# A cross network of six layers: four sums of a middle layer's state made by accumulating DMAs in place of VectorE

## The chip, the core and the metric

The kernel runs on one core of one Trainium2 chip. The metric is the device time of one launch in microseconds (us), given as the median of several runs. Beside it there is a trace of one profiled execution; all durations below come from that trace.

## What is computed

The reference is a deep cross network on 16384 rows of 1024 bf16 values, with six layers. The state starts as x0; each layer multiplies the state by its own 1024x1024 weight, adds a bias, multiplies the result element by element with x0 and adds the old state:

```python
B, Din, L = 16384, 1024, 6
x = x0
for l in range(L):
    proj = jnp.einsum('bd,de->be', x, ws[l]) + bs[l]
    x = x0 * proj + x
return x
```

The last line of the loop is what the change is about: the sum of the new product and the old state.

## The kernel before

**Tiling.** The 16384 rows are cut into 16 pairs of two blocks of 512 rows. The state of a pair is held transposed in SBUF, 128 partitions by (n, k, b): n is the block (0 or 1), k one of eight slices of 128 features, b the row. Its two halves of features are called eh = 0 (k 0 to 3) and eh = 1 (k 4 to 7). So a state has four quarters of 128x2048 values (512 KB in bf16), one for each n and eh.

**Loops.** The outer loop `s` runs over eight outer steps, each with two pairs, called side A and side B. Inside it `l` runs over the six layers, and in each layer first A and then B is a step: 96 steps in all. The two sides alternate so that one side's last sums can be made while TensorE works on the other.

**Strassen products.** In each step the 2x2 block product of features by blocks of rows is made in Winograd's way from seven products instead of eight, numbered by `pid` (1, 2, 3 on parts of the state itself; 5, 6, 7, 4 on differences of them, the tiles `T13`, `T2` and `T4`). From the second outer step on, products 2 and 4 are in turn made from seven smaller ones, on differences in the tiles `ti2` and `ti4`. `mm` (L403) issues a product's matmuls of 128x512, `inner` (L411) those of 128x256. ScalarE brings the results from PSUM to the SBUF tiles P1s, S53 (the profile's S), P5s, U2s, C2 (the profile's cb), ea, eb and e4.

**The sums of a state.** Four products with x0 and four sums with the old state make the new state `xst` of a pair:
- quarter (n 0, eh 0) from P1s, by `m0` and `a0` near the end of the pair's own step;
- quarter (n 1, eh 0) from S53, by `m1` and `a1` in the following step, which is the other side's;
- quarters (n 1, eh 1) and (n 0, eh 1) from the two halves of C2, by one product and one sum over both, `mC2` and `aC2`, also in the following step.

`trail(Y, store)` returns the operations of the previous pair Y that are still to be made; `fin_of` gives a product and a sum of one quarter. In layers after the first the old state and the new one are the same tile (`X.src = X.xst` at a step's end), so the sum is made in place.

**Order.** All engines keep the order in which the program issues (`keep_in_program_order`). A step of VectorE goes: T13 of the step's own side; then the previous pair's operations mixed with T2, T4 and the ti4 differences, in the order of the list at L441; then the sums of ea and eb, and P1s + ea; then, by the list at L556, the ti2 differences of the other side's next step mixed with m0 and a0; then U2s + S53. The ti2 differences of the next step read the quarter (n 0, eh 1) that `aC2` has written in this step; the other side's T13 at the head of the next step reads the other three quarters.

**Buffers.** P1s, S53, P5s and U2s have one buffer each, C2 has two. So ScalarE can't fill P1s in a step before the product and the sum of the step before have read it. The weights are in a ring of nine tiles of 512 KB, one for each `pid` and for the two inner sets; SP loads the next layer's tile into a slot as soon as side B has used it. SP also loads the next x0 with transposing DMAs (from the second outer step to the seventh in layers 2 and 3, side A), and turns and writes finished states in the steps of layers 5 and 0. GpSimd issues nothing after the first few us.

Of the kernel before, what the change touches and what calls it, by code (L numbers as in the profile page):

```python
# [8 lines left out]
ADD = mybir.AluOpType.add  # L9
SUB = mybir.AluOpType.subtract  # L10
MULT = mybir.AluOpType.mult
# [6 lines left out]
def kernel(  # L18
# [7 lines left out]
    nc = tc.nc  # L26
    P = nc.NUM_PARTITIONS
    B, D = x0.shape
    L = ws.shape[0]
    KD = D // P  # L30
    KH = KD // 2
# [11 lines left out]
    pin = tc.keep_in_program_order  # L43

    def vtt(out, in0, in1, op):
        return pin(nc.vector.tensor_tensor(out=out, in0=in0, in1=in1, op=op))  # L46

    def vcopy(out, in_):
        return pin(nc.vector.tensor_copy(out=out, in_=in_))
# [23 lines left out]
    def evt(name):  # L73
        return ev_pool.tile([P, KH, NB], BF16, name=name)
# [47 lines left out]
    def combo(l, pid):  # L122
        if pid <= 7:
            a, op, b = {5: (lambda: raw12[l], ADD, lambda: W[0, l, 4]), 6: (lambda: W[0, l, 5], SUB, lambda: W[0, l, 1]),
                        3: (lambda: W[0, l, 2], SUB, lambda: W[0, l, 6]), 7: (lambda: W[0, l, 1], SUB, lambda: raw12[l])}[pid]
            if pid == 5:
                W[0, l, 5] = ei_pool.tile([P, KH, H], BF16, name=("eb", "e4")[l % 2])
            t = W[0, l, pid]
            vtt(t[:], a()[:], b()[:], op)
        else:  # L130
            w = W[0, l, {8: 2, 9: 4}[pid]]
            t = W[0, l, 8] if pid == 8 else ti_pool.tile([P, KH, H], BF16, name="ti4")
            i11, i12, i21, i22 = w[:, 0:2, 0:HE], w[:, 0:2, HE:H], w[:, 2:4, 0:HE], w[:, 2:4, HE:H]
            iv = t[:].rearrange("p k (j e) -> p k j e", e=HE)
            vtt(iv[:, 0], i12, i22, ADD)
            vtt(iv[:, 3], i11, i12, SUB)
            vtt(iv[:, 1], iv[:, 0], i11, SUB)
            vtt(iv[:, 2], i21, iv[:, 1], SUB)
        pin(nc.sync.dma_start(lc(l, pid), t[:]))

    def sub4(t):
        return {(i, j): t[:, 2 * i:2 * i + 2, j * NQ:(j + 1) * NQ] for i in range(2) for j in range(2)}

    def inner_t(hold, src, name):

        def t02():
            ti = ti_pool.tile([P, 4, 2, NQ], BF16, name=name)
            setattr(hold, name, ti)
            b = sub4(src())
            vtt(ti[:, 0], b[0, 1], b[0, 0], SUB)  # L150
            vtt(ti[:, 2], b[1, 1], b[0, 1], SUB)

        def t1():
            ti = getattr(hold, name)
            vtt(ti[:, 1], sub4(src())[1, 1], ti[:, 0], SUB)

        def t3():
            ti = getattr(hold, name)
            vtt(ti[:, 3], sub4(src())[1, 0], ti[:, 1], SUB)

        return [t02, t1, t3]
# [96 lines left out]
    def half(eh):  # L258
        return slice(eh * KH, (eh + 1) * KH)

    def trail(Y, store):

        if Y is None:
            return [None] * 7
        C2, E4, e5 = Y.C2, Y.E4, Y.e5
        eh1 = lambda t: t[:, :, KH:KD, :]
        m1, a1 = fin_of(Y, Y.C12, 0, 1)

        def s4():
            for i in range(2):  # L270
                vtt(E4[:, 2 * i:2 * i + 2, NQ:NB], E4[:, 2 * i:2 * i + 2, (1 - i) * NQ:(2 - i) * NQ], e5[:], ADD)

        def a1s():
            a1()
            if store:
                store_half(Y, 0)

        return [m1, lambda: vtt(C2[:, 1], C2[:, 1], Y.P5s[:], ADD), a1s,
                s4 if E4 is not None else None,
                (lambda: vtt(C2[:, 0], C2[:, 0], E4[:], ADD)) if E4 is not None else None,  # L280
                lambda: vtt(C2[:], C2[:], eh1(Y.x0T), MULT),
                lambda: vtt(eh1(Y.xst), C2[:], eh1(Y.src_in), ADD)]

    def fin_of(Y, C, eh, n):
        xs = half(eh)
        return [lambda: vtt(C, C, Y.x0T[:, n, xs, :], MULT),
                lambda: vtt(Y.xst[:, n, xs, :], C, Y.src_in[:, n, xs, :], ADD)]

    def fin_rows(X, C, n, eh, js=slice(0, KH), state=None):
# [17 lines left out]
    def store_half(Y, eh):  # L307
        ks = half(eh)
        for n in range(2):
            pin(nc.sync.dma_start_transpose(out=Y.x0T[:, n, ks, :].rearrange("p k (j r) -> p (k j) r", r=P),  # L310
                                            in_=Y.xst[:, n, ks, :].rearrange("r k b -> r (k b)")))
        with nc.allow_non_contiguous_dma(reason="256B runs"):
            for n in range(2):
                r0 = Y.pr * PR + n * NB
                for j in range(KH):
                    pin(nc.sync.dma_start(
                        out[r0 + j * P:r0 + (j + 1) * P, eh * H:(eh + 1) * H].rearrange("p (k r) -> p k r", r=P),
                        Y.x0T[:, n, ks, j * P:(j + 1) * P]))
# [12 lines left out]
    for s in range(NPAIR // 2):  # L331
        for l in range(L):
            for side in ("A", "B"):
                X, Y = cur[side], prev
                first, last = step == 0, (X.pr, l) == LAST
                in2, in4 = not first, s > 0 and not (s + 1 == NPAIR // 2 and l + 1 == L)
                psA, psX = ps[step % 2], ps[1 - step % 2]
                step += 1
                bias = lambda eh, m, l=l: b_all[:, l * KD + eh * KH + m: l * KD + eh * KH + m + 1]
# [83 lines left out]
                        abias(dst[:, m, :], pts[m][:], bias(eh, m))  # L423

                ended = Y is not None and Y.l == L - 1
                m1, s11, a1, s4, e4, mC2, aC2 = trail(Y, ended and last)
                if not first:
                    X.T13()
                P1s = evt("P1s")
# [8 lines left out]
                ev(P1s, pA, 0, 0)  # L438
                t2, t4 = (None, None) if first else (X.T2, X.T4)
                i02, i1, i3 = inner_t(X, lambda: X.T[4], "ti4") if in4 else [None] * 3  # L440
                for f in (m1, s11, a1, t2, s4, t4, e4, i02, mC2, i1, aC2, i3):  # L441
                    if f is not None:
                        f()
                if in2:
# [4 lines left out]
                    P5s, S53 = evt("P5s"), evt("S53")  # L449
# [53 lines left out]
                else:  # L503
# [20 lines left out]
                    P5s, S53 = evt("P5s"), evt("S53")  # L524
# [24 lines left out]
                if first:  # L549
                    combo(0, 8)  # L550
                m0, a0 = fin_of(X, P1s[:], 0, 0)
                j02, j1, j3 = inner_t(N, lambda: N.rhs(2), "ti2") if need2 else [None] * 3
                if last:
# [24 lines left out]
                U2s = evt("U2s")  # L578
                X.E4 = X.e5 = X.defer = None
                C2 = cb_pool.tile([P, 2, KH, NB], BF16, name="cb")  # L580
                X.C2, X.P5s, X.l = C2, P5s, l
                if in4:
                    w4, w4i, w7 = weights(4), weights(9), weights(7)
                    wj, wr4 = w4i[:].rearrange("p k (j e) -> p k j e", e=HE), sub_w(w4, HE)
                    b4, t4 = sub4(X.rhs(4)), X.ti4
                    E4 = X.E4 = ei_pool.tile([P, KH, NB], BF16, name="e4")
                    X.e5 = ei_pool.tile([P, 2, NQ], BF16, name="e5")
                    e4 = sub4(E4)
# [104 lines left out]
```

## Time and profile before

| | us |
|---|---|
| median of 3 runs | 2268.25 (2268.05 to 2268.64) |
| the profiled execution, its own time | 2268.03 |
| its span in the trace | 2266.2 |
| TensorE busy | 2259.2 (100%) |
| VectorE busy | 2161.6 (95%) |
| ScalarE busy | 1910.9 (84%) |
| GpSimd busy | 0.7 |
| DMA, share of 16 engines (SP's queue) | 51.7% |
| granted TensorE clock | 1.00 of full speed |

The span is the time from the first to the last instruction in the trace; 1.8 us of the execution lie around it. An engine's idle time matters only where the chain of work that ended last runs through it. A step's length can be read from one `T<-big 128x4096` of VectorE, the T13 at the head of each step, to the next.

### The profile page before, as it was taken

The numbers are of one execution on the slowest core, as the hardware profiler recorded it, in microseconds if no ns is written. First come the engines' busy times: TensorE is split into PE (matmuls) and PEld (weight loads), VectorE is DVE, ScalarE is ACT, GpSimd is POOL, SyncE is SP. The second block draws the span as 40 slices with busy tenths as digits, with TensorE's granted clock in tenths as the row PEclk, the third lists the DMA queues.
The fourth block names the chain that finished last, engine by engine and source line by source line (L and its number), as shares of the span: only waits on it lengthen the run. The fifth ranks groups of instructions, "written<-read, shape, count | busy, mean of one in ns | idle before, by whom it ended". The sixth has DMA issues, their size and how long they took to land.

```text
span 2266.2 us, 33559 instructions
## 1 busy us (share of the span) xinstructions
PE 2259.2 (100%) x12925; PEld 1264.4 (56%) x12925; DVE 2161.6 (95%) x2394; ACT 1910.9 (84%) x3307; POOL 0.7 (0%) x6
## 2 busy tenths in 40 slices
PE   9999999999999999999999999999999999999999
PEld 4555555555555555555555555555555555555554
DVE  8999989999999999999999999999999999999999
ACT  6777788888888888888888888888888888888887
POOL 0000000000000000000000000000000000000000
PEclk9999999999999999999999999999999999999999
DMA  7423494523945239442494434944348443483337
GB/s 231 151 94 121 149 216 159 146 85 119 255 133 136 93 124 257 132 121 97 128 259 122 121 112 127 245 121 121 125 124 236 121 131 121 126 228 121 104 119 178
DMA packets 508452, 334.59 MB, mean 148 GB/s; under 512 B 390530, under 2 KB 470404, under 8 KB 508292
## 3 DMA queue, kind: packets, MB, share of 16 engines
q1 hardware_dynamic: 508292, 332.45, 51.7%
q8 instruction: 101, 1.65, 0.3%
q14 instruction: 59, 0.48, 0.1%
HBM read 213.92 MB, written 52.43 MB: 118 GB/s over the span
## 4 chain that ended last, share of the span: by engine, by line
PE 99%; DMA 0%; DVE 0%; SPq 0%; issue 0%; ACT 0%; DVEq 0%
PE px L403 74%; PE px L411 24%; PE px L398 1%; DMA wp<-in_ws_dram 0%; DVE cb L46 0%; SPq L120 0%; DVE eb L46 0%; DVE T L46 0%; DVE wp L46 0%; SPq L217 0%; PE px L395 0%; PE px L393 0%; ACT cb L52 0%; SPq L220 0%; DVEq L46 0%
## 5 line engine op out<-in xcount | busy, mean ns | idle before, releaser
L403 PEld LDWEIGHTS <-wp 128*128 128x128 bf16 x7344 | 718.5, 98 | 669.9 <-issue 0.8
L403 PE MATMUL px<-T,wp 128*128 128x512 bf16 x4384 | 1069.4, 379 | 0.0
L403 PE MATMUL px<-big,wp 128*128 128x512 bf16 x2960 | 712.4, 379 | 0.4 <-ACT big L52 0.4
L411 PEld LDWEIGHTS <-wp 128*128 128x128 bf16 x4752 | 465.0, 98 | 254.3
L55 ACT ACTIVATE cb<-px,b_all 128x512 bf16<-128x512 f32 x760 | 502.0, 686 | 85.3 <-PE px L403 71.4
L411 PE MATMUL px<-ti,wp 128*128 128x256 bf16 x2684 | 402.7, 273 | 0.0
L52 ACT CAST ea<-px 128x512 bf16<-128x512 f32 x344 | 201.6, 586 | 140.5 <-PE px L411 140.5
L46 DVE TENSOR_TENSOR T<-big 128x4096 bf16<-128x4096 bf16 (+1 forms) x97 | 220.1, 2269 | 71.0 <-PE px L403 71.0
L52 ACT CAST U2s<-px 128x512 bf16<-128x512 f32 x384 | 225.0, 586 | 64.4 <-PE px L403 61.4
L55 ACT ACTIVATE P1s<-px,b_all 128x512 bf16<-128x512 f32 x380 | 254.3, 695 | 6.0 <-PE px L403 4.4
L55 ACT ACTIVATE S<-px,b_all 128x512 bf16<-128x512 f32 x380 | 242.3, 703 | 0.8 <-PE px L403 0.8
L46 DVE TENSOR_TENSOR T<-big,T 128x2048 bf16<-128x2048 bf16 x192 | 234.1, 1219 | 1.4
L52 ACT CAST P5s<-px 128x512 bf16<-128x512 f32 x384 | 217.9, 596 | 17.7 <-PE px L403 17.5
L46 DVE TENSOR_TENSOR cb<-cb,big 128x4096 bf16<-128x4096 bf16 (+2 forms) x105 | 221.6, 2113 | 0.7 <-ACT cb L52 0.5
L46 DVE TENSOR_TENSOR big<-cb,big 128x4096 bf16<-128x4096 bf16 x95 | 217.2, 2286 | 0.5
L52 ACT CAST e<-px 128x512 bf16<-128x512 f32 x328 | 192.7, 588 | 0.0
L411 PE MATMUL px<-big,wp 128*128 128x256 bf16 x1084 | 162.6, 273 | 0.0
L52 ACT CAST eb<-px 128x512 bf16<-128x512 f32 x258 | 152.1, 590 | 6.2
L411 PE MATMUL px<-T,wp 128*128 128x256 bf16 x984 | 134.2, 273 | 0.0
L46 DVE TENSOR_TENSOR P1s<-P1s,big 128x2048 bf16<-128x2048 bf16 x106 | 129.3, 1220 | 3.3 <-ACT P1s L55 2.4
L46 DVE TENSOR_TENSOR S<-U2s,S 128x2048 bf16<-128x2048 bf16 (+1 forms) x97 | 117.2, 1208 | 2.5 <-ACT U2s L52 2.4
L46 DVE TENSOR_TENSOR S<-S,big 128x2048 bf16<-128x2048 bf16 (+1 forms) x99 | 118.5, 1197 | 0.1
(77 smaller groups left out, 1360.8 us busy)
## 6 DMA issues: line engine op xcount, KB each, us to landing
wp<-Lc SPq DMA_DIRECT2D x252, 512.0 KB, 4.6
wp<-in_ws_dram SPq DMA_DIRECT2D x144, 512.0 KB, 3.4
out_dram<-big SPq DMA_DIRECT2D x28, 1024.0 KB, 10.7
Lc<-big SPq DMA_DIRECT2D x15, 512.0 KB, 2.7
Lc<-wp SPq DMA_DIRECT2D x9, 512.0 KB, 2.7
ea<-in_ws_dram SPq DMA_DIRECT2D x6, 512.0 KB, 5.2
Lc<-ti SPq DMA_DIRECT2D x6, 512.0 KB, 3.1
big<-in_x_dram SPq DMA_DIRECT2D x1, 2048.0 KB, 9.9
```

What stands on the lines that cost most here:

```text
L46: return pin(nc.vector.tensor_tensor(out=out, in0=in0, in1=in1, op=op))
L52: return pin(nc.scalar.copy(out=out, in_=in_))
L55: return pin(nc.scalar.activation(out=out, in_=in_, func=IDENT, bias=bias, scale=1.0))
L398: nc.tensor.matmul(pt, lhsT=rhs[:, k, m * P:(m + 1) * P], rhs=wt[:, k, :], start=(start and k == 0 and pid != 1), stop=(k == KH - 1), **kw)
L403: nc.tensor.matmul(pts[m][:], lhsT=wt[:, k, m * P:(m + 1) * P], rhs=rhs[:, k, :], start=(start and k == 0), stop=(k == KH - 1), **kw)
L411: nc.tensor.matmul(dst(m), lhsT=w[:, k, m * P:(m + 1) * P], rhs=rhs[:, k, :], start=(start and m == 0 and k == 0), stop=(k == 1), skip_gro ...
```

## The change

In layers 1 to 4 each of the four sums becomes a DMA that GpSimd issues. Its source is the product, its destination the quarter of the state, and it adds what it brings to what is there. The two products on the halves of C2 are made one by one instead of together, each directly behind the operation that completes its half, and each is followed by its own DMA; so the product of half 0 stands ahead of the ti4 differences, where the common product stood among them. The sum a1 has become a DMA directly behind m1, and a0 one at its old place between the ti2 differences. Layers 0 and 5 keep VectorE's sums: in layer 0 the old state is x0 in another tile, and layer 5 goes on to the output.

In the rebuilt order of the engines TensorE, ScalarE and SP issue the same instructions in the same order as before, and GpSimd issues 256 further DMAs of 128x2048, four in each of 64 steps.

```diff
+    def dadd(out, in_):
+        return pin(nc.gpsimd.dma_start(out=out, in_=in_, accum_op=ADD))
...
     def trail(Y, store):
...
-        return [m1, lambda: vtt(C2[:, 1], C2[:, 1], Y.P5s[:], ADD), a1s,
+        mul = lambda n: vtt(C2[:, n], C2[:, n], Y.x0T[:, n, KH:KD, :], MULT)
+        acc = lambda n: dadd(Y.xst[:, n, KH:KD, :], C2[:, n])
+
+        def m2():
+            mul(1)
+            acc(1)
+
+        def m3():
+            mul(0)
+            acc(0)
+
+        dma = by_dma(Y)
+        return [m1, a1s if dma else None, lambda: vtt(C2[:, 1], C2[:, 1], Y.P5s[:], ADD), m2 if dma else None, None if dma else a1s,
                 s4 if E4 is not None else None,
-                (lambda: vtt(C2[:, 0], C2[:, 0], E4[:], ADD)) if E4 is not None else None,
-                lambda: vtt(C2[:], C2[:], eh1(Y.x0T), MULT),
-                lambda: vtt(eh1(Y.xst), C2[:], eh1(Y.src_in), ADD)]
+                (lambda: vtt(C2[:, 0], C2[:, 0], E4[:], ADD)) if E4 is not None else None, m3 if dma else None,
+                None if dma else lambda: vtt(C2[:], C2[:], eh1(Y.x0T), MULT),
+                None if dma else lambda: vtt(eh1(Y.xst), C2[:], eh1(Y.src_in), ADD)]
+
+    def by_dma(Y):
+        return 0 < Y.l < L - 1
 
     def fin_of(Y, C, eh, n):
         xs = half(eh)
         return [lambda: vtt(C, C, Y.x0T[:, n, xs, :], MULT),
+                (lambda: dadd(Y.xst[:, n, xs, :], C)) if by_dma(Y) else
                 lambda: vtt(Y.xst[:, n, xs, :], C, Y.src_in[:, n, xs, :], ADD)]
...
-                m1, s11, a1, s4, e4, mC2, aC2 = trail(Y, ended and last)
+                m1, d1, s11, m2, a1, s4, e4, m3, mC2, aC2 = trail(Y, ended and last)
...
-                for f in (m1, s11, a1, t2, s4, t4, e4, i02, mC2, i1, aC2, i3):
+                for f in (m1, d1, s11, m2, a1, t2, s4, t4, e4, m3, i02, mC2, i1, aC2, i3):
```

In what follows d1 is the DMA behind m1 (from S53), d2 and d3 those behind the products on the halves 1 and 0 of C2, and d0 the one that stands for a0 (from P1s).

More of the change, by code (lines that the diff above doesn't have):

```diff
@@ L263, in trail @@
         if Y is None:
-            return [None] * 7
+            return [None] * 10
         C2, E4, e5 = Y.C2, Y.E4, Y.e5
@@ L336 @@
                 in2, in4 = not first, s > 0 and not (s + 1 == NPAIR // 2 and l + 1 == L)
+                X.l = l
                 psA, psX = ps[step % 2], ps[1 - step % 2]
@@ L580 @@
                 C2 = cb_pool.tile([P, 2, KH, NB], BF16, name="cb")
-                X.C2, X.P5s, X.l = C2, P5s, l
+                X.C2, X.P5s = C2, P5s
                 if in4:
```

## The prediction

> **What bounds the kernel now.** I read the page first, then one step of VectorE and of ScalarE in the timeline, then the DMA share by windows, then the DMA issues. The page:
>
> ```profile
> PE 2259.2 (100%) x12925; PEld 1264.4 (56%) x12925; DVE 2161.6 (95%) x2394; ACT 1910.9 (84%) x3307; POOL 0.7 (0%) x6
> ...
> PE 99%; DMA 0%; DVE 0%; SPq 0%; issue 0%; ACT 0%; DVEq 0%
> ```
>
> TensorE is busy for 2259.2 of 2266.2 us and carries 99% of the chain that ended last. What VectorE gives up can therefore buy at most the 7.0 us in which TensorE is idle, all of it, by the windows, in the first 30.5 (28.12 busy) and the last 55.2 us (50.58). VectorE is nearly as full. One step of it (layer 3, side A) in the timeline, start and duration in us:
>
> ```profile
> 995.27 2.29 DVE L46 TENSOR_TENSOR T<-big 128x4096 bf16<-128x4096 bf16 x1 [0.84 <-PE px L403]
> ...
> 999.75 1.22 DVE L46 TENSOR_TENSOR big<-S,big 128x2048 bf16<-128x2048 bf16 x1
> ...
> 1008.17 2.28 DVE L46 TENSOR_TENSOR big<-cb,big 128x4096 bf16<-128x4096 bf16 x1
> ...
> 1015.11 1.22 DVE L46 TENSOR_TENSOR big<-P1s,big 128x2048 bf16<-128x2048 bf16 x1
> ...
> 1018.65 2.29 DVE L46 TENSOR_TENSOR T<-big 128x4096 bf16<-128x4096 bf16 x1 [0.84 <-PE px L403]
> ```
>
> A step lasts 23.38 us (995.27 to 1018.65), as nearly all steps do; VectorE waits in it for 0.84 us alone, for TensorE. The sums are the three forms that write big: 1.14 + 2.20 + 1.14 us from start to start (a 128x2048 takes 1.14, a 128x4096 2.20, two 128x512 0.67). ScalarE in that step:
>
> ```profile
> 998.38 1.27 ACT L55 ACTIVATE P1s<-px,b_all 128x512 bf16<-128x512 f32 x2
> ...
> 1002.64 0.59 ACT L52 CAST ea<-px 128x512 bf16<-128x512 f32 x1 [0.71 <-PE px L411]
> ...
> 1004.38 0.59 ACT L52 CAST ea<-px 128x512 bf16<-128x512 f32 x1 [0.17 <-PE px L411]
> ...
> 1008.47 0.69 ACT L55 ACTIVATE P1s<-px,b_all 128x512 bf16<-128x512 f32 x1
> ```
>
> P1s has one buffer: ScalarE fills it from 3.11 us after the step's T (998.38 - 995.27) to 13.89. The cast of ea at 1004.38 ends at 1004.97 and TensorE reuses its bank at 1005.04, so a late ScalarE stops TensorE once its idle 0.71 + 0.17 and that 0.07, 0.95 us, are used up. The DMA share (second number from the right) of the two steps of one layer, then of 10.9 to 16.9 us after T in a B step, in an A step of layers 2 and 3, and in one of layer 4:
>
> ```profile
> 784.85:808.23 23.38, 23.38 (x138) 13.31 (x137) 22.43 (x26) 20.10 (x36) 0.00 (x0) 1.00 0.40 135
> 808.23:831.61 23.38, 23.38 (x138) 13.29 (x137) 22.43 (x26) 20.10 (x36) 0.00 (x0) 1.00 0.19 68
> 1029.55:1035.55 6.00, 6.00 (x32) 2.99 (x31) 5.90 (x7) 5.65 (x12) 0.00 (x0) 1.00 0.91 298
> ...
> 1006.17:1012.17 6.00, 6.00 (x32) 2.99 (x31) 5.90 (x7) 5.65 (x12) 0.00 (x0) 1.00 0.72 158
> 1052.93:1058.93 6.00, 6.00 (x32) 2.99 (x31) 5.90 (x7) 5.65 (x12) 0.00 (x0) 1.00 0.01 3
> ```
>
> A layer's nine weight loads (512 KB each) take (0.40 + 0.19) x 23.38 = 13.8 us of all 16 engines, 1.53 each. They crowd into the middle of the B steps; in the A steps of layers 2 and 3 it is the transposing loads of the next x0. From issue to landing:
>
> ```profile
> wp<-Lc SPq DMA_DIRECT2D x252, 512.0 KB, 4.6
> ...
> Lc<-big SPq DMA_DIRECT2D x15, 512.0 KB, 2.7
> ```
>
> **What is removed.** In the 64 steps of layers 1 to 4, sums of 1.14 + 1.14 + 2.20 = 4.48 us leave VectorE; two 128x2048 products in place of one 128x4096 give back 0.08. Its idle time grows from 0.84 to 5.2 us a step. TensorE's, ScalarE's and SP's orders stay, so this alone is worth nothing.
>
> **What is added.** 256 accumulating DMAs of 512 KB, four a step, all in GpSimd's queue, each behind its own product; GpSimd has nothing else to do. In us after a step's T: product with S ends at 3.42 (d1 goes out), C2[1]'s at 5.69 (d2), C2[0]'s, now ahead of the inner T4 differences, at 2.20 + 3 x 1.14 + 1.14 (T2) + 0.67 + 1.14 (T4) + 1.14 + 1.22 = 10.9 (d3). Behind it VectorE does the ti4 differences (1.34), ea (1.13) and P1s + ea, which waits for P1s until 13.89, and comes at 15.03 to the ti2 differences of the other side's next step. These read the half of the state that d3 writes. This is the new wait: queued behind it are P1s x x0, whose DMA (d0) goes out 0.67 + 1.22 us later, U2s + S, and the next T; and ScalarE can't fill P1s in the next step, at 23.38 + 3.11 = 26.49, before d0 has read it.
>
> **The price of a wait.** Let L3 and L0 be the times from the product's end to the landing. Up to L3 = 15.03 - 10.9 = 4.1 nothing waits. Above it d0 lands at 10.9 + L3 + 1.89 + L0, and TensorE stops when this passes 26.49 + 0.95: when L3 + L0 is over 14.65 us, and by the excess, in each such step. The other deadlines are looser: VectorE's own circle (next T at 23.38, 3.64 us of work behind the wait) allows L3 = 8.9, S is refilled at 12.6 (d1 may take 9.2), d2 has until the next T. A weight tile is freed one step (23.38 us) ahead of its next use and lands in 4.6, so weights have some 18 us of cover; if that went, TensorE would wait for wp.
>
> **How long a landing takes.** No row shows an accumulating DMA. Fixed part: 2.7 (Lc<-big) less 1.53 of moving is 1.2 us; GpSimd's handing over lies between SP's issue of such a DMA (0.32 to 0.38) and SP's slowest (5.1 for a transposing load, 10.28 for two). I take 1.8, a third of the way, as the form is that of the former and the engine neither's: f = 3.0. Moving: the addend and the old state are both read, so between one copy, 1.53, and three, 4.6; I take the middle, two, c = 3.06. Where another queue has work, I let it take turns, so time doubles.
> - B steps (28, outer steps 1 to 7): d1 and d2 need 6.1, and loads 2.1 (share 0.28), of the 7.5 us ahead of d3, which starts 0.7 late; L3 = f + 2c + 0.7 = 9.8, L0 = f + c = 6.1, sum 15.9: 1.25 us over, 35 us in all.
> - A steps of layers 2 and 3 in outer steps 1 to 6 (12): loads fill the engines (share up to 1.14) until about 15, where d1 and d2 have had 5.5 of their 6.1; d3 moves to 18.7 and lands at 21.7: L3 = 10.8, L0 = 6.1, sum 16.9, 2.25 over, 27 us.
> - The 16 other A steps of outer steps 1 to 7: 2 x 6.1 = 12.2, hidden with 2.4 to spare. The first outer step, whose loads lie otherwise: 0 (at most 8 x 1.25 = 10).
>
> Sum 62 us on the profiled 2268.0 (span 2266.2 and 1.8 around it; the median is 2268.25): **2330**. With one copy all is hidden, 2268. With c = 4.0 the same sums give 5.95 over in the 40 steps, 238 us, 2506; with 4.6, 8.95 and 8.35 over there and 2.25 in the 16 free A steps, some 390 us, 2660. Below nothing the 7.0 us of idle TensorE are the limit.
>
> **A rule that gives another result.** The row is 2.7 us for a plain 512 KB. The Trainium skill (DMA: Bandwidth & Descriptors, section Anatomy of one DMA) fits a GpSimd-issued DMA as 2.0 us plus bytes over 436 GB/s; with both operands counted that makes an estimated 4.4 us, f = 2.0 and c = 2.4, and by it a B step's sum is 11.2 and nothing is lost. No run here shows such a DMA.
>
> **Rivals.**
> - *Hidden after all* (the other side): landings short enough that L3 + L0 stays under 14.65 everywhere; with f = 3.0 this holds in the B steps from c under 2.8, in the crowded A steps from 2.5. For it: the point lies just under my c, and the uncrowded steps have 2.4 us to spare. Against: six of the eight crossings of a layer cycle are crowded. 2268. The rule above gives this.
> - *The DMA engines fill up*: two steps need 13.8 + 8c of 46.76 us, so from c = 4.1 on the loads fall behind, whatever the waits. At 4.6: (50.6 - 46.76) / 2 = 1.9 us in 64 steps at the least, with the waits above 2390 to 2660. Against: a copy takes 1.53.
> - *GpSimd can hand over only while VectorE pauses*: nothing in the trace speaks on it, as GpSimd is idle. d3 would wait for 15.03 (4.1 later), d0 0.7: 4.8 more in each sum, 6.0 and 7.0 over in the crowded steps, 2.4 in the 16 free ones, 292 us: 2560. The Trainium skill (SBUF — State Buffer, section Summary: rules for kernel authors) has GpSimd's descriptor writing starved while VectorE runs in its 2x mode; the same page's section on interference exempts two-input operations, which is what these are.
> - *A gain*: only the 7.0 us; at the ends the layers are 0 and 5, which the change leaves out.
>
> **How the numbers follow.** Waits as summed, 0.44; hidden 0.27; engines full 0.16; handing over held up 0.10; gain 0.03. A change of 0.2% (4.5 us) is about what a measurement tells from none: faster 0.03, same 0.27, slower 0.70. The range reaches from 2265, hidden and a little less, to 2510, c of 4.0; the likeliest case alone holds 2275 to 2510.
>
> **What would show it.** Right: VectorE loses 4.5 us a step, its wait ahead of ti<-big is for the DMA, ScalarE waits at P1s for a DMA, and the steps of outer steps 1 to 7 longer than 23.38 us are the B steps and the A steps of layers 2 and 3. Wrong: all steps at 23.38 (hidden), TensorE waiting for wp (engines full), or landings over 10 us in the free A steps (handing over).

## The result, and the profile after

The changed kernel takes 2780.07 us (median of 4 runs, 2771.76 to 2809.77) against 2268.26 us before (4 runs, 2268.05 to 2268.64): a ratio of 1.228, with a 95% interval of 1.221 to 1.235. The prediction had the direction and named two of the three waits, but the loss is 512 us where it forecast 62, far beyond its range.

The page of the profiled execution (2771.76 us, span 2769.9); the lines that the change adds shift the numbers, so L424 and L432 are the former L403 and L411, the matmuls of `mm` and `inner`, L56 and L59 ScalarE's former L52 and L55, and L50 is the new DMA:

```profile
PE 2352.4 (85%) x12925; PEld 1293.5 (47%) x12925; DVE 1906.4 (69%) x2266; ACT 1901.6 (69%) x3307; POOL 221.0 (8%) x262
...
PEclk9999998899979999879998899978999888999999
...
q0 software_dynamic: 36864, 134.23, 27.9%
...
PE 54%; DMA 26%; DVE 6%; ACT 3%; issue 1%; another core or an unknown queue 1%; DVEq 0%; POOL 0%; ACTq 0%; POOLq 0%
PE px L424 38%; PE px L432 15%; DMA big<-S 12%; DMA big<-cb 9%; DMA big<-P1s 5%; DVE T L46 1%; DVE cb L46 1%; DVE ti L46 1%; DVE S L46 1%; DVE P1s L46 1%; ACT P1s L59 1%; ACT ea L56 1%; PE px L419 1%; ACT P5s L56 0%
```

TensorE, 2259.2 us busy before, is now idle for 2769.9 - 2352.4 = 417.5 us instead of 7.0. The other 93 us of the loss are in its busy time: the same 12925 matmuls run longer, because the granted clock falls in and after the stalls, as a window below shows. A quarter of the chain now consists of the new DMAs, and the largest share is d1's, `big<-S`.

The waits by engine (us in all, times, longest) name three chains:

```profile
ACT S L59 <- DMA big<-S: 291.5, 15, 34.8
PE px L432 <- ACT S L59: 260.8, 11, 32.7
...
DVE ti L46 <- DMA big<-cb: 218.8, 42, 9.3
...
ACT P1s L59 <- DMA big<-P1s: 168.0, 27, 8.1
```

The second and third DMA waits are those that the prediction worked with (d3 ahead of the ti2 differences, d0 ahead of the refill of P1s). The first is the deadline it had set aside as looser: ScalarE can't refill S53 before d1 has read it. It comes only 15 times, and costs TensorE 260.8 us in 11 stalls.

From T13 to T13, in us, summed by kind of step (A and B are the sides, the number is the layer, s the outer step; measured minus the same steps of before):

| steps | predicted | measured |
|---|---|---|
| 2A, 3A of s = 1 to 6 (12, the next x0 is loaded) | 27 | 357 |
| 1B to 4B of s = 1 to 7 (28) | 35 | 59 |
| 4A, 5A of s = 1 to 7; 2A, 3A of s = 7 (16) | 0 | 78 |
| s = 0 | 0 | 9.5 |
| all | 62 | 503.7 |

So one step in eight carries 70% of the loss. One of them, 2A of s = 3, in the timeline, together with what its waits waited for:

```profile
1093.21 2.28 DVE L46 TENSOR_TENSOR T<-big 128x4096 bf16<-128x4096 bf16 x1
...
1093.59 47.06 SPq L232 DMA_TRANSPOSE big<-in_x_dram  x2
...
1097.16 0.86 POOL L50 DMA_DIRECT2D big<-S  x1 [4.32 <-issue]
...
1101.11 1.26 ACT L59 ACTIVATE P1s<-px,b_all 128x512 bf16<-128x512 f32 x2 [6.83 <-DMA big<-P1s]
...
1133.88 0.69 ACT L59 ACTIVATE S<-px,b_all 128x512 bf16<-128x512 f32 x1 [23.37 <-DMA big<-S]
...
1134.62 1.01 PE L432 MATMUL px<-T,wp 128*128 128x256 bf16 x4 [21.28 <-ACT S L59]
...
1145.43 2.29 DVE L46 TENSOR_TENSOR T<-big 128x4096 bf16<-128x4096 bf16 x1 [2.05 <-PE px L424]
```

SP's two transposing loads, whose issuing holds SP for 10.28 us in such a step before, hold it for 47.06. GpSimd hands d1 over at 1097.16 in 0.86 us, and S53 is free only 36.6 us later. TensorE stands for 21.28 us. The windows of that stall and of what follows it (length, then busy time of PE, PEld, DVE, ACT and POOL, granted clock, DMA share, GB/s), then one of before in which such a load runs alone, and the packets of SP's queue (q1: packets, MB, share of the engines' time) in that stretch of before and in the stall:

```profile
1112.31:1134.62 22.31, 1.03 (x5) 0.39 (x4) 0.00 (x0) 0.74 (x2) 0.00 (x0) 0.59 1.21 80
1134.62:1140.47 5.85, 5.85 (x20) 2.96 (x20) 2.43 (x4) 4.73 (x9) 0.00 (x0) 0.51 1.19 123
...
1005.00:1010.00 5.00, 5.00 (x26) 2.44 (x25) 5.00 (x6) 4.16 (x8) 0.00 (x0) 1.00 1.11 245
```

```profile
q1 hardware_dynamic: 4791, 1.21, 109.9%
...
q1 hardware_dynamic: 2105, 0.53, 67.6%
```

In the stall the DMA engines count as more than full (1.21) and move 80 GB/s. A share over 1 isn't new: a load by itself had 1.11 before, but moved 245. What is new is the time of a packet. The loads' packets hold some 253 bytes in both stretches; before, one took 1.099 x 16 x 5.00 us / 4791 = 18 ns, in the stall 0.676 x 16 x 22.31 us / 2105 = 115 ns. Time on the engines and bytes moved have come apart. In the 5.85 us after it TensorE is busy throughout at a clock of 0.51: the price of a stall is more than its length. The Trainium skill (TensorE: Matmul & The Clock Gate, Why this matters for your kernels) has TensorE fall to half rate after a gap of some 3 us. This trace agrees as far as it goes, with 0.51 after a gap of 21.28 us; where the limit lies, this window can't show.

The pair of steps without loads shows the other two chains, here 4B and 5A of s = 3, first the timeline, then the chain of waits (start, length, what):

```profile
1292.98 0.86 POOL L50 DMA_DIRECT2D big<-cb  x1 [4.48 <-ACT P5s L56]
...
1302.73 0.76 DVE L46 TENSOR_TENSOR ti<-big 128x512 bf16<-128x512 bf16 x2 [6.29 <-DMA big<-cb]
...
1305.25 0.86 POOL L50 DMA_DIRECT2D big<-P1s  x1 [11.41 <-DVE ti L46]
...
1314.89 1.26 ACT L59 ACTIVATE P1s<-px,b_all 128x512 bf16<-128x512 f32 x2 [6.99 <-DMA big<-P1s]
...
1316.68 1.01 PE L432 MATMUL px<-ti,wp 128*128 128x256 bf16 x4 [5.10 <-ACT ea L56]
```

```profile
1292.98 9.65 DMA big<-cb
...
1302.73 0.76 DVE ti L46 x2
1303.49 1.14 DVE P1s L46
...
1305.25 9.53 DMA big<-P1s
...
1314.89 1.26 ACT P1s L59 x2
```

That is the predicted path link by link: d3, the ti2 differences, P1s x x0, d0, the refill of P1s, TensorE.

### The profile page after: what moved, and what is told of

It is laid out like the page before. It is cut to its first block, busy times and chain, and to the rows that moved or that the text cites. A ratio compares the mean times of both kernels' runs of the same rounds, so it can differ in the third digit from the quotient of the medians.

```text
span 2769.9 us, 34275 instructions
## 1 busy us (share of the span) xinstructions
PE 2352.4 (85%) x12925; PEld 1293.5 (47%) x12925; DVE 1906.4 (69%) x2266; ACT 1901.6 (69%) x3307; POOL 221.0 (8%) x262
## 4 chain that ended last, share of the span: by engine, by line
PE 54%; DMA 26%; DVE 6%; ACT 3%; issue 1%; another core or an unknown queue 1%; DVEq 0%; POOL 0%; ACTq 0%; POOLq 0%
PE px L424 38%; PE px L432 15%; DMA big<-S 12%; DMA big<-cb 9%; DMA big<-P1s 5%; DVE T L46 1%; DVE cb L46 1%; DVE ti L46 1%; DVE S L46 1%; DVE P1s L46 1%; ACT P1s L59 1%; ACT ea L56 1%; PE px L419 1%; ACT P5s L56 0%
## 5 line engine op out<-in xcount | busy, mean ns | idle before, releaser
L424 PE MATMUL px<-T,wp 128*128 128x512 bf16 x4384 | 1115.2, 391 | 4.5 <-DVE T L46 2.7
L424 PEld LDWEIGHTS <-wp 128*128 128x128 bf16 x7344 | 730.5, 100 | 701.2 <-issue 36.4
L432 PEld LDWEIGHTS <-wp 128*128 128x128 bf16 x4752 | 481.9, 101 | 689.4 <-issue 437.4
L424 PE MATMUL px<-big,wp 128*128 128x512 bf16 x2960 | 712.3, 379 | 0.4 <-ACT big L56 0.4
L59 ACT ACTIVATE cb<-px,b_all 128x512 bf16<-128x512 f32 x760 | 501.6, 686 | 84.3 <-PE px L424 70.0
L432 PE MATMUL px<-ti,wp 128*128 128x256 bf16 x2684 | 428.0, 285 | 139.3 <-ACT ea L56 139.3
L59 ACT ACTIVATE S<-px,b_all 128x512 bf16<-128x512 f32 x380 | 241.8, 701 | 292.3 <-DMA big<-S 291.5
L59 ACT ACTIVATE P1s<-px,b_all 128x512 bf16<-128x512 f32 x380 | 253.8, 693 | 211.7 <-DMA big<-P1s 168.0
L46 DVE TENSOR_TENSOR P1s<-P1s,ea 128x2048 bf16<-128x2048 bf16 x86 | 105.4, 1225 | 409.5 <-ACT P1s L59 406.2
L432 PE MATMUL px<-T,wp 128*128 128x256 bf16 x984 | 138.8, 279 | 260.8 <-ACT S L59 260.8
L56 ACT CAST ea<-px 128x512 bf16<-128x512 f32 x344 | 202.8, 589 | 158.3 <-PE px L432 158.1
L56 ACT CAST U2s<-px 128x512 bf16<-128x512 f32 x384 | 225.0, 590 | 65.9 <-PE px L424 62.9
L46 DVE TENSOR_TENSOR ti<-big 128x512 bf16<-128x512 bf16 x190 | 71.9, 420 | 263.9 <-DMA big<-cb 218.8
L46 DVE TENSOR_TENSOR cb<-cb,big 128x2048 bf16<-128x2048 bf16 (+3 forms) x169 | 232.0, 1374 | 4.7 <-ACT cb L56 0.5
L56 ACT CAST P5s<-px 128x512 bf16<-128x512 f32 x384 | 218.0, 596 | 17.5 <-PE px L424 17.3
L50 POOL DMA_DIRECT2D big<-P1s x64 | 55.2, 863 | 1752.2 <-ACT U2s L56 833.7
L56 ACT CAST e<-px 128x512 bf16<-128x512 f32 x328 | 193.6, 590 | 0.5 <-PE px L432 0.4
L432 PE MATMUL px<-big,wp 128*128 128x256 bf16 x1084 | 175.1, 287 | 0.0
L56 ACT CAST eb<-px 128x512 bf16<-128x512 f32 x258 | 153.6, 595 | 4.3 <-PE px L432 0.2
```

The source lines that it names most:

```text
L50: return pin(nc.gpsimd.dma_start(out=out, in_=in_, accum_op=ADD))
L56: return pin(nc.scalar.copy(out=out, in_=in_))
L59: return pin(nc.scalar.activation(out=out, in_=in_, func=IDENT, bias=bias, scale=1.0))
L424: nc.tensor.matmul(pts[m][:], lhsT=wt[:, k, m * P:(m + 1) * P], rhs=rhs[:, k, :], start=(start and k == 0), stop=(k == KH - 1), **kw)
L432: nc.tensor.matmul(dst(m), lhsT=w[:, k, m * P:(m + 1) * P], rhs=rhs[:, k, :], start=(start and m == 0 and k == 0), stop=(k == 1), skip_gro ...
```

## The experiments

What was open: why d1 takes 36 us in the steps that load, and whether the two kinds of loss are separate. One theory has the transposing loads and GpSimd's DMAs slow each other far beyond sharing. Its rivals: the accumulating DMA is slow by itself; GpSimd can't hand over; the single buffers of P1s and S53 alone are too few.

**The loads moved (e1).** The next x0 is loaded in 1A and 5B instead of 2A and 3A.

```diff
-                    if l == (2 if s > 0 else L - 1):
+                    if l == (1 if s > 0 else L - 1):
...
-                    if l == 3 and s > 0:
-                        pending.append(lambda: bring("B"))
+                if side == "B" and l == L - 1 and 0 < s and s + 1 < NPAIR // 2:
+                    bring("B")
```

> The changed kernel, with the transposing loads of the next x0 moved out of layers 2 and 3 to steps in which no accumulating DMA is in flight: side A's to layer 1, side B's to layer 5 of the step's own side B. Theory 1 (a transposing load and an accumulating DMA hold each other up when both are in flight): the A steps of layers 2 and 3, now 24 to 67 us long, become like those of layers 4 and 5, some 28 to 30 us; 357 us of loss in 12 steps shrink to about 60, so some 2475 us. Theory 2 (the DMA engines simply have too many bytes, as in the prediction's rival): the same bytes move, so the time stays within 50 us of 2772.

Measured: 2597.29 us (2589.26 to 2611.07), ratio 1.146 (1.141 to 1.150). The steps 2A and 3A lose 5.5 us each now, no more than the other A steps. But 5A, which has d1 to d3 of layer 4, loses 16 to 34 us in s = 1 to 6, 156 in all. Windows of a 2A and a 5A, and the timeline in that 5A:

```profile
1066.28:1095.55 29.27, 24.48 (x123) 13.09 (x125) 18.56 (x25) 18.19 (x34) 3.44 (x4) 0.88 0.60 141
1227.82:1285.36 57.54, 26.28 (x121) 13.58 (x122) 19.61 (x26) 17.86 (x33) 2.58 (x3) 0.70 1.18 98
```

```profile
1228.37 53.33 SPq L232 DMA_TRANSPOSE big<-in_x_dram  x2
...
1274.27 0.69 ACT L59 ACTIVATE S<-px,b_all 128x512 bf16<-128x512 f32 x1 [28.47 <-DMA big<-S]
```

My edit was wrong in place: SP has nothing to wait for and issued the loads written in 5B at the start of 5A. The miss is as telling as a hit: the loss goes where the loads go, with the same wait for d1.

**Two buffers for P1s (e2).** The tile of P2s, which is unused from the second outer step on, takes P1s in every other step.

```diff
-                P1s = evt("P1s")
+                P1s = evt("P1s" if step % 2 else "P2s")
```

> The changed kernel with two buffers for P1s (the tile P2s, which only the first step uses, takes every other step). If the path of the prediction is the one that costs the 5 us in the A steps of layers 4 and 5 (C2's half 0 lands late, so P1s's DMA goes out late and ScalarE waits to refill P1s), these steps fall back to about 23.4 us and the loss outside the A steps of layers 2 and 3 (some 147 us) nearly goes; those steps still wait for S: 2560 to 2640 us. If P1s only stands in for the next wait (S, or VectorE at the ti2 differences), under half of the 147 goes: over 2680.

Measured: 2676.17 us (one run). Windows of 4A, 4B and 5A, then of a 2A:

```profile
1221.84:1242.41 20.57, 20.41 (x116) 11.53 (x118) 18.47 (x24) 17.22 (x31) 3.47 (x4) 1.00 0.70 159
1242.41:1267.55 25.14, 25.03 (x149) 14.49 (x149) 18.40 (x24) 21.86 (x38) 3.46 (x4) 1.00 0.82 213
1267.55:1289.17 21.62, 21.46 (x123) 12.12 (x124) 19.51 (x25) 18.19 (x33) 2.59 (x3) 1.00 0.72 164
1065.62:1119.61 53.99, 24.26 (x122) 12.89 (x123) 18.56 (x25) 18.20 (x34) 3.45 (x4) 0.72 1.19 107
```

TensorE's longest kind of wait (us in all, times, longest):

```profile
PE px L432 <- ACT S L59: 361.3, 12, 44.4
```

Without loads an A and a B step average 23.4 us again, at full clock: d3 still makes VectorE late (25.14), but d0 no longer holds ScalarE, and TensorE runs through. So the d0 chain cost what stood outside the loading steps, and a late T13 by itself costs nothing. The loading steps still lose 370 us, and TensorE's 12 long stalls, one for each of them, are all behind S53, which waits for d1. The two losses have separate causes. The time is over the 2560 to 2640 us of the first case, because the loading steps lose more than the 357 us of the change, and because the B steps ahead of them pass on some 2 us each that isn't made up there.

**Both (e3).** The edits of e1 and e2 together.

> Both edits together: loads moved, and two buffers for P1s. If the two causes are all there is, 2268 to 2285 us, no step over 24 us. If a third one is left (the S tile's single buffer, VectorE's own circle through the landing of C2's half 0), 2300 to 2400 us.

Measured: 2434.23 us (2420.84 to 2462.52), ratio 1.071 (1.066 to 1.076). That is above both ranges. A 2A (first line) is free of any loss, and the misplaced loads' 5A (second line) carries most of what is left: 167 us of 194.5 in the profiled run, which is the longest of the four, with 27 to 39 us in each of s = 1 to 4 and 6, and 6.6 in s = 5:

```profile
1021.75:1043.27 21.52, 21.36 (x122) 12.02 (x123) 18.47 (x25) 18.26 (x34) 3.45 (x4) 1.00 0.75 177
1162.11:1224.11 62.00, 23.13 (x121) 12.51 (x123) 19.52 (x26) 18.07 (x33) 2.59 (x3) 0.70 1.21 91
```

**Copies in place of accumulation (e4).** The changed kernel, with its 256 DMAs as plain ones, so that the old state isn't added in layers 1 to 4.

```diff
-        return pin(nc.gpsimd.dma_start(out=out, in_=in_, accum_op=ADD))
+        return pin(nc.gpsimd.dma_start(out=out, in_=in_))
```

> The changed kernel with plain DMAs of GpSimd in place of the accumulating ones: same source, destination, waits and order, but the old state is not read and not added in layers 1 to 4, which leaves that part of the computation out. If the second read is what makes a landing long (3.0 us of engine time, as two copies), a DMA takes 1.5 us of engine time and lands in about 3.5 to 4 where it is quiet, and steps without transposing loads go back to 23.4 us. For the A steps of layers 2 and 3: if adding is what clashes with the transposing loads, they lose under 5 us each and the whole takes 2270 to 2330; if any DMA issued by GpSimd clashes, they still lose 15 to 30 each and the whole takes 2450 to 2620.

Measured: 2395.82 us (one run), between the two ranges. The DMA issues and queues of the page (the last number of an issue is the median from issue to landing):

```profile
q0 software_dynamic: 36864, 134.23, 16.1%
...
big<-cb POOLq DMA_DIRECT2D x128, 512.0 KB, 4.8
big<-P1s POOLq DMA_DIRECT2D x64, 512.0 KB, 2.9
```

A copy takes 0.161 x 2394.0 / 256 = 1.51 us of all 16 engines, an accumulation (the page after) 0.279 x 2769.9 / 256 = 3.02: twice that. From the second outer step on nearly all steps are back at 23.4 us or a little under, except 2A and 3A of s = 1 to 6, which lose 134 us, 5.6 to 15.4 each. So accumulating makes the clash worse, but isn't its source: plain DMAs from GpSimd clash with the loads too, for over a third of the 357 us.

**Loads without transposition (e5).** The loads of x0 from the third pair on become plain ones of the same 1 MB; those pairs get a rearranged x0.

```diff
-            pin(nc.sync.dma_start_transpose(out=x0T[:, n], in_=x0[r0:r0 + NB, :]))
+            if pr < 2:
+                pin(nc.sync.dma_start_transpose(out=x0T[:, n], in_=x0[r0:r0 + NB, :]))
+            else:
+                pin(nc.sync.dma_start(out=x0T[:, n].rearrange("p k b -> p (k b)"),
+                                      in_=x0[r0:r0 + NB, :].rearrange("(p r) d -> p (r d)", p=P)))
```

> The changed kernel with the x0 loads of the pairs from the third on made as plain loads (1 MB each, not transposed, so these pairs get rearranged input; everything else is as in the changed kernel). If it is the transposing that clashes, a load lands in about 6 to 12 us in place of 27, the A steps of layers 2 and 3 lose no more than those of layers 4 and 5 (about 5 us), and the time is 2430 to 2490 us. If any load from SP of that size clashes, these steps still lose 20 us or more and the time is over 2650.

Measured: 2482.06 us (one run), with the loads at the same places as in the change. Windows of a 2A, which loads, and a 4A, which doesn't:

```profile
1017.35:1046.14 28.79, 23.41 (x123) 12.71 (x124) 18.73 (x24) 18.14 (x33) 3.44 (x4) 0.88 0.78 215
1126.63:1154.86 28.23, 22.63 (x115) 12.26 (x117) 18.55 (x25) 16.91 (x32) 3.45 (x4) 0.88 0.59 130
```

They are alike: what is left in both is the d0 chain. In the profiled runs the loading steps lose 62 us in place of 357. The loads land in 15.4 us (median), longer than the 6 to 12 I had written down, but no stall comes of it: the same bytes at the same time, loaded plainly, cost these steps no more than the others. One thing besides the transposition differs: the packets. In 1018 to 1030 us of this run SP's queue moves 2.50 MB in 647 packets, 3.9 KB each (one weight tile included), where the transposing loads have some 253 bytes. So this run doesn't tell whether the transposition clashes or the small packets that come with it.

**The clash by itself (m1).** The kernel before, with four independent copies of 512 KB to DRAM of a tile that nothing else uses, in 2A and 3A of s = 1 to 6, by three issuers in turn:

```diff
+                if side == "A" and l in (2, 3) and 0 < s < NPAIR // 2 - 1:
...
+                    for i in range(4):
...
+                        if s in (3, 4):
+                            pin(nc.scalar.dma_start(to, still[:]))
+                        elif s in (1, 2):
+                            pin(nc.gpsimd.dma_start(to, still[:]))
+                        else:
+                            pin(nc.gpsimd.dma_start(out=to, in_=still[:], accum_op=ADD))
```

> The kernel before (VectorE's sums) with four DMAs of 512 KB, of an unused tile to an unused place in DRAM, added right behind T in the A steps of layers 2 and 3, on which no other work waits: plain ones of GpSimd in outer steps 1 and 2, plain ones of ScalarE in 3 and 4, accumulating ones of GpSimd in 5 and 6. Read: the time from issue to landing of the transposing loads, 7.1 us in the kernel before. If a second queue's traffic as such slows them, they take 15 us or more in all six; if what GpSimd issues does, 8 to 11 in 3 and 4 and over 15 in the others; if only adding does, over 15 in 5 and 6 alone. The time as a whole stays within 40 us of 2268, as the loads have a step or more of cover.

Measured: 2287.25 us (one run). The DMA issues by stretches of two outer steps, from issue to landing:

```profile
scr<-P2s POOLq DMA_DIRECT2D x16, 512.0 KB, 19.6
big<-in_x_dram SPq DMA_TRANSPOSE x10, 18.6
...
scr<-P2s ACTq DMA_DIRECT2D x16, 512.0 KB, 9.7
big<-in_x_dram SPq DMA_TRANSPOSE x8, 12.1
...
scr<-P2s POOLq DMA_DIRECT2D x16, 512.0 KB, 24.8
big<-in_x_dram SPq DMA_TRANSPOSE x8, 26.2
```

In the kernel before, the loads of the same stretches land in 7.7, 6.3 and 7.1 us. These medians mix a step's first load, which has the copies beside it, with its second, which often hasn't, and the first stretch (x10) holds two loads of layer 0 without any copies. The time for which a step's two loads hold SP is the better measure; here one step of each kind, from the timeline (GpSimd's copies, ScalarE's, accumulating):

```profile
389.78 25.41 SPq L229 DMA_TRANSPOSE big<-in_x_dram  x2
...
950.90 17.44 SPq L229 DMA_TRANSPOSE big<-in_x_dram  x2
...
1522.14 42.45 SPq L229 DMA_TRANSPOSE big<-in_x_dram  x2
```

| the four DMAs are | SP held before | if they shared fairly | measured, four steps |
|---|---|---|---|
| GpSimd's copies (s = 1, 2) | 10.8 to 11.6 | 16.8 to 17.7 | 23.6 to 37.1 |
| ScalarE's copies (s = 3, 4) | 10.2 to 10.9 | 16.3 to 16.9 | 17.2 to 19.0 |
| GpSimd's accumulations (s = 5, 6) | 10.6 to 12.4 | 22.7 to 24.4 | 26.0 to 42.5 |

Fair sharing adds four copies of 1.51 us or four accumulations of 3.02. ScalarE's copies nearly fit that (their median landing of 12.1 is a little over the 8 to 11 I had written down); GpSimd's don't, though the first of them goes out some 1.2 us later in its step than ScalarE's. So the clash needs none of the change's waits, and the same copy does more harm from GpSimd than from ScalarE.

**Loads in their place (e6), and no DMAs in the first outer step (e7).** e6 is e3 with the loads of side B held back into 5B, a step in which GpSimd issues nothing:

```diff
-                    bring("B")
+                    pending.append(lambda: bring("B"))
```

> As the run with both edits, but side B's loads go out in the step of layer 5, side B, where the last accumulating DMA of the outer step has long landed. In the run before, SP issued them one step earlier than meant, into the A step of layer 5, and that step alone then lost 26 to 38 us. Theory 1 (transposing loads and accumulating DMAs hold each other up): every step of outer steps 1 to 7 averages 23.4 us, what is left is the first outer step's 8 to 10 us: 2274 to 2285 us. If layer 5's A step loses for a reason of its own, it still does: over 2400.

e7 takes the first outer step out as well (`X.s` is kept beside `X.l`):

```diff
-        return 0 < Y.l < L - 1
+        return Y.s > 0 and 0 < Y.l < L - 1
```

> As the one before, with the accumulating DMAs only from the second outer step on; the first keeps VectorE's sums. If the rest of 8 to 10 us comes from the first outer step's own loads and stores beside the accumulating DMAs, it goes: 2266 to 2271 us, the same as before the change. If it is lost elsewhere, 2274 to 2285.

Measured: e6 2286.68 us (2284.95 to 2289.20), ratio 1.008 (1.007 to 1.010); e7 2277.32 us (2275.08 to 2279.27), ratio 1.0038 (1.0024 to 1.0052). e6 lies just above its range, e7 in its second one, for a rest that is lost elsewhere. The loads in e6, in the timeline of a 5B, take their 10 us again, and the steps of s = 1 to 5 average 23.38 us:

```profile
1129.22 10.39 SPq L232 DMA_TRANSPOSE big<-in_x_dram  x2
```

e6 loses 10.5 us in s = 0, which e7 has back; what e7 still loses lies elsewhere (see the end of the next section). So 493 of the 512 us went in e6 with two edits that leave all 256 accumulating DMAs as they are.

**The loads left, the DMAs moved (e8).** Two buffers for P1s, the loads in 2A and 3A as in the change, no DMAs in s = 0 nor, for side B, in layers 1 and 2, so that d1 to d3 are gone from the loading steps (168 DMAs remain).

```diff
-        return 0 < Y.l < L - 1
+        return Y.s > 0 and (Y.l in (3, 4) or Y.l in (1, 2) and Y.pr % 2 == 0)
```

> The other way round: the transposing loads stay in layers 2 and 3, and the accumulating DMAs keep away from them. From the second outer step on, side A's sums of layers 1 to 4 and side B's of layers 3 and 4 are DMAs (168 of the 256); side B's of layers 1 and 2, which would go out in the A steps of layers 2 and 3, stay on VectorE. P1s has two buffers. Theory 1: nothing is left that meets a transposing load, 2266 to 2275 us. If the number of accumulating DMAs counts, and not their meeting the loads, two thirds of the changed kernel's loss stay: about 2600; with P1s's part taken off, about 2500.

Measured: 2279.69 us (2278.35 to 2283.43), ratio 1.0056 (1.0039 to 1.0073): the large loss is gone this way too, from the other side, though the time is a little over the range I gave.

**The edits without the DMAs (c3).** The kernel before, with the loads as in e6 and two buffers for P1s.

> The kernel before with VectorE's sums, the transposing loads moved as in the run with side B's loads placed right, and two buffers for P1s: what these two edits cost by themselves. 2268 us if the rest of 9 to 18 us in the runs with moved loads belongs to the accumulating DMAs; 2275 or more if moving the loads costs it.

Measured: 2268.96 us (2268.09 to 2270.10), ratio 1.0003 (0.9994 to 1.0013). The edits cost nothing, so what e7 and e8 still lose against before belongs to the DMAs.

## Why the prediction was wrong

**Right: the bound.** TensorE's order carried the time, and VectorE's freed time bought nothing. VectorE gave up 2161.6 - 1906.4 = 255 us, forecast (4.48 - 0.08) x 64 = 282; where the difference lies was not looked into. Even e7, with VectorE at 1935.9 us, is slower than before.

**Right: the moving time c.** 3.06 taken, 3.02 measured; as it was the middle of a bracket from 1.53 to 4.6, the hit is partly luck. **Nearly right: f.** In quiet, in a step of layer 1 on side A, d0 lands 4.5 us after its issue (issued at 1064.50), so 1.5 are fixed, and 0.86 us of handing over, not 1.8, lie inside it; 3.0 was too much. The fit of the Trainium skill (DMA: Bandwidth & Descriptors, Anatomy of one DMA), 4.4, agrees with that landing; its result, nothing lost, doesn't follow, as hardly any landing is quiet.

**Right as a formula, wrong in a term: L3 + L0.** For 4B and 5A above, d3's product ends some 0.6 us ahead of the issue at 1292.98, and the ti2 differences start at 1302.73: L3 is 10.3 (forecast 9.8). d0's product ends at 1304.7 and P1s is refilled at 1314.89: L0 is 10.2 (forecast 6.1). The sum, 20.5, is 5.85 over the point of 14.65; TensorE's stall is 5.10. The mis-sized term is L0: I let d0 go alone, but at the head of a layer's A step it meets other work. The timeline has SP issue three weight loads between 1304.67 and 1307.16 and GpSimd d1 and d2 of the next step at 1310.42 and 1312.81, all ahead of d0's landing; no run separates them. The loss of a B step also falls due in the A step behind it, with a clock of 0.88 there. That is why the 28 B steps and the 16 A steps behind them lose 59 + 78 us, forecast 35 + 0. e2 shows this chain by removing it, and e4, with landings of 2.9 us (median) for d0, has no such loss either.

**Wrong by more than ten times: the loading steps (27 us forecast, 357 measured).** The step that failed is "Where another queue has work, I let it take turns, so time doubles", with its result that the loads fill the engines until about 15 us after T. Two loads of 10.28 us together, four accumulations of 3.02 and three weight loads of 1.53 are 27 us of work; the loads alone held SP for 47.06. I treated the share of the engines as a currency that any two queues can spend. m1 shows that this nearly holds for ScalarE's copies and not for GpSimd's; e4 that accumulation makes the loss 2.7 times as large but isn't needed; e5 that with plain loads there is none; e1, e6 and e8 that it goes with the overlap in time.

**Wrong with it: the "looser" deadlines.** With a landing of 36.6 us, the allowance of 9.2 for d1 was the first to break, as d1 is handed over directly after the loads. I had compared the allowances with one assumed landing, not with one that could be several times as long.

**The rivals.** *Handing over held up*: wrong; handing over takes 0.86 us each, and d1 of 3B in s = 2, issued at 875.56, lands 4.59 us later, of which VectorE is busy for 4.56. *The DMA engines fill up*: not as written; the engines' share is over 1 in the loading steps, but TensorE's stalls are behind S53 and P1s (260.8 and 139.3 us), not weights. *Hidden*: of the steps with such a DMA, right in 1A alone, and nearly so everywhere once the loads are elsewhere and P1s has two buffers.

**Open.** Why a DMA issued by GpSimd and a transposing load slow each other beyond sharing isn't shown by these traces: they show packets of 253 bytes that take 115 ns in place of 18, not what holds them up. Whether it is the transposition or the small packets isn't shown either, as no run has small packets of another kind beside GpSimd's DMAs. Another issuer for the accumulating DMAs was not tried. Nor is the last 0.4% of e7 settled: of 9.3 us in the profiled run 6.7 lie in s = 6 and 7, 2.1 behind the last T13 and 0.6 in the first step of s = 0, and of TensorE's waits for a DMA the longest are two short ones for a weight tile (from the waits of e7):

```profile
PE px L432 <- DMA wp<-Lc: 2.2, 2, 1.3
```

No version beats the kernel before, and the reason is the first line of its page: what was unloaded was not the bound.

## What to carry to other kernels

Before work is moved to DMAs, list which other transfers share its time, and by kind, not by the share of the engines alone; a transposing load on one queue and DMAs issued by GpSimd are better kept apart in time, for the place of the loads alone was worth 389 us here (e2, a single run, to e6). A DMA that reads a working buffer holds that buffer until it lands, so it needs a second buffer or a deadline well above its quiet landing (here 4.5 us in quiet and 36.6 beside the loads). And price a stall of TensorE above its length, for the matmuls behind it ran slower too (93 us on top of 410 of added idle time).

## What was unexpected in the hardware

- The issuer matters to the other queue: beside the same four copies of 512 KB, a step's two transposing loads hold SP for 17.2 to 19.0 us when ScalarE issues the copies and for 23.6 to 37.1 when GpSimd does, from 10.2 to 11.6 without them. The Trainium skill (DMA: Bandwidth & Descriptors, Issuing engines are not separate DMA queues) says that DMAs from all issuers interleave on the same engines, whichever engine started them. How long the loads take does depend on the issuer in this run (m1).
- Both sides suffer: the page of after has the loads at a median of 26.5 us (7.1 before), while d1 in such steps takes 13 to 51 (median 40), and in the stall shown the whole core moves 80 GB/s.
- An accumulating DMA costs twice a copy in engine time (3.02 and 1.51 us for 512 KB), and in quiet lands in 4.5 us against some 2.9.
- 93 of 504 us of loss are matmuls at a lower granted clock (0.51 in the 5.85 us after a stall of 21.28).
